# Three blocks in halves in place of four, and twelve slots per step with round ends drawn forward, in a fused convolution and two-matmul kernel

## The chip, the cores and the metric

The kernel runs on one core of a Trainium2 chip. The metric is the device time of one execution in microseconds (us). A span is the profiled part of an execution; it is mostly some 1.7 us shorter than the time. The **chain** of a profile is the work that ended last, followed back from the last instruction to what released each piece.

## The reference, cut to what matters

```python
# x: (8, 4096, 192), weight: (8 heads, 7 taps), w_in: (192, 2048), w_out: (2048, 192)
w = softmax(weight)                       # over the taps
y[b, s, :] = sum over k of w[head, k] * x_pad[b, s + k, :]   # causal, 7 taps
h = y.reshape(32768, 192) @ w_in          # first matmul
g = np.maximum(0.01 * h, h)
out = g @ w_out                           # second matmul
```

## The kernel before

The tokens are cut into 32 blocks (512 positions of two batch rows each). VectorE makes the convolution of a block (`yt`), TensorE the first matmul into PSUM (`ph`, two buffers), ScalarE (ACT in the profile) the activation into `g`, and TensorE the second matmul, which lags behind by some groups. Its outputs (`po`, `acc`) have four buffers in PSUM. A **group** is one half block or one whole block.

The first four blocks are processed as eight half blocks, so that work starts early. In this first stage, and in the first whole block after it, the second matmul has the form of `mm2_row_slot`: a **slot** is two matmuls on two halves of the array rows, and sixteen slots are a **round**. Between the two rounds of a pair of outputs the row halves swap outputs, and the program makes the swap wait for a copy on ACT (`seal`). From the second whole block on, the other form (`mm2_slot`, L545) is used, with 48 slots of four matmuls per block.

```python
NHALF = 4                                  # blocks in halves
groups = [(b, h * HT, HT) for b in range(NHALF) for h in range(2)]
groups += [(b, 0, ST) for b in range(NHALF, NBLK)]      # HT = 256, ST = 512
NSW = 2 * NHALF                            # the first whole block

def mm1(grp, u, M):                        # one unit: matmuls into ph, one activation
    ph = psum_h.tile([128, 2, ST], FP32, name="ph", tag="ph")     # bufs=2
    ...                                    # 12 matmuls of 256 or 6 of 512 columns (M=128)
    nc.scalar.activation(out=g[blk][...], in_=ph..., func=Prelu, alpha=0.01)

def mm2_row_slot(q):
    p, fc = divmod(q, 2 * NFC)             # NFC = 16: a pair has two rounds of 16 slots
    rnd, fc = divmod(fc, NFC)
    ...
    for rt in range(2):
        ins = mm2_one(rt, pair[rt ^ rnd], fc, ...)
        if first and rnd == 1:
            sync(ins, seal, "both row tiles have left these banks")
    if last and rnd == 0:
        seal_round(p, ins)                 # a copy on ACT (of the pair before, if any)
    if last and rnd == 1:
        evac_o(pair[0])                    # a copy on ACT

plan = {
    0: [0] * 4,
    NSW - 2: [16, 8, 8, 16],
    NSW - 1: [8, 8, 16, 16],
    NSW: [16, 8, 8, 16, 8, 8, 16, 16],
}
for i, grp in enumerate(groups):
    ...
    quota = plan.get(i, [16] * 4 if T == HT else [5, 5, 6, 5, 5, 6, 8, 8])
    for j in range(steps):                 # 4 steps in a half block, 8 in a whole one
        for u in range(2 * j, 2 * j + 2):
            mm1(grp, u, 128 if i <= NSW else CH)
        ...                                # whole blocks: convolution jobs of the next group
        for _ in range(quota[j]):
            mm2_row_slot(slot) if i <= NSW else mm2_slot(slot)
            slot += 1
        ...
```

The total of slots in the last three groups of the first form is 192 in 16 steps, twelve per step on average. Before, they are dealt as 16, 8, 8, 16 so that every round ends at the end of a step.

## Time and profile before

| | |
|---|---|
| time | 686.46 us (685.19 to 686.69, 3 runs) |
| TensorE busy | 99% of the span; 97% of the chain |
| ACT busy | 77%; 2% of the chain |
| VectorE busy | 71% |
| half-block group | 10.52 us with 64 slots, 9.45 us with 48 |
| whole block, later form | 20.72 us |

The last two rows come from the busy time per stretch. Each row names a stretch in us, its length, then each engine's busy time with its number of instructions (PE is TensorE, PEld its weight loads, DVE VectorE, then ACT, and POOL for GpSimd), the granted clock, the DMA share and GB/s:

```profile
51.04:61.56 10.52, 10.52 (x230) 10.52 (x226) 10.20 (x28) 9.02 (x13) 4.46 (x6) 1.00 0.66 88
72.08:81.53 9.45, 9.39 (x198) 9.20 (x194) 6.56 (x12) 8.60 (x12) 4.46 (x6) 1.00 0.84 89
192.93:213.65 20.72, 20.72 (x392) 13.20 (x388) 15.04 (x24) 15.89 (x18) 4.45 (x6) 1.00 0.60 78
```

The first is group 4 (16 slots per step), the second group 6 (16, 8, 8, 16), the third a steady whole block. In the first and third TensorE is busy the whole stretch; in the second it has 0.06 us without work.

### The profile page before, as it was taken

The numbers are of one execution on the slowest core, as the hardware profiler recorded it, in microseconds if no ns is written. First come the engines' busy times: TensorE is split into PE (matmuls) and PEld (weight loads), VectorE is DVE, ScalarE is ACT, GpSimd is POOL, SyncE is SP. The second block draws the span as 40 slices with busy tenths as digits, with TensorE's granted clock in tenths as the row PEclk, the third lists the DMA queues.
The fourth block names the chain that finished last, engine by engine and source line by source line (L and its number), as shares of the span: only waits on it lengthen the run. The fifth ranks groups of instructions, "written<-read, shape, count | busy, mean of one in ns | idle before, by whom it ended". The sixth has DMA issues, their size and how long they took to land.

```text
span 683.4 us, 27404 instructions
## 1 busy us (share of the span) xinstructions
PE 677.7 (99%) x12575; PEld 464.4 (68%) x12575; DVE 482.5 (71%) x844; ACT 524.6 (77%) x624; POOL 146.0 (21%) x204
## 2 busy tenths in 40 slices
PE   9999999999999999999999999999999999999998
PEld 6999986666666666666666666666666666666667
DVE  7979758667687667687667786676876676876612
ACT  7888998777777777777778777777777778777781
POOL 7722222222102222112221022221022220000000
PEclk9999999999999999999999999999999999999999
DMA  9975668557466566565564665574665664321123
GB/s 155 93 101 76 84 79 98 61 60 94 78 89 81 60 73 92 80 90 74 56 84 79 87 92 68 56 93 79 89 82 64 69 91 75 72 55 34 34 49 93
DMA packets 211763, 53.29 MB, mean 78 GB/s; under 512 B 205120, under 2 KB 211264, under 8 KB 211648
## 3 DMA queue, kind: packets, MB, share of 16 engines
q0 software_dynamic: 98736, 13.97, 29.9%
q1 hardware_dynamic: 112896, 37.57, 27.8%
q8 instruction: 98, 1.61, 1.0%
q14 instruction: 17, 0.14, 0.1%
q10 hardware_dynamic: 16, 0.00, 0.0%
HBM read 28.31 MB, written 25.17 MB: 78 GB/s over the span
## 4 chain that ended last, share of the span: by engine, by line
PE 97%; ACT 2%; DVE 0%; issue 0%; ACTq 0%
PE ph L456 48%; PE acc L545 41%; PE po L482 7%; ACT g L463 2%; PE acc L228 1%; ACT yt L415 0%; ACT L330 0%; ACTq L259 0%; ACT diag L387 0%; DVE yt L247 0%; ACT xt L172 0%; DVE o_sb L593 0%; DVE x_half L137 0%; ACT w L336 0%; ACT junk L330 0%
## 5 line engine op out<-in xcount | busy, mean ns | idle before, releaser
L463 ACT ACTIVATE g<-ph 128x1024 bf16<-128x1024 f32 x512 | 496.2, 1021 | 137.0 <-PE ph L456 136.6
L206 DVE SCALAR_TENSOR_TENSOR yt<-xt,wk,yt 128x512 bf16<-128x512 bf16 (+1 forms) x618 | 383.5, 702 | 0.2
L456 PE MATMUL ph<-yt,w_in 64*64 64x512 bf16 (+2 forms) x6048 | 378.4, 363 | 1.3 <-ACT g L463 0.6
L545 PE MATMUL acc<-g,w_out 64*64 64x512 bf16 x5184 | 316.5, 376 | 0.0
L456 PEld LDWEIGHTS <-w_in 64*64 64x64 bf16 (+1 forms) x6048 | 238.0, 129 | 99.1 <-issue 3.8
L545 PEld LDWEIGHTS <-w_out 64*64 64x64 bf16 x5184 | 166.7, 118 | 110.2
L82 POOL DMA_DIRECT2D x_bf<-in_x_dram x180 | 134.2, 770 | 416.2 <-DMA xt<-x_bf 309.9
L567 DVE STREAM_TRANSPOSE o_t<-acc 128x512 f32<-128x512 f32 x81 | 68.1, 885 | 169.5 <-PE acc L545 169.5
L482 PE MATMUL po<-w_out,g 64*128 64x192 bf16 (+1 forms) x1152 | 60.1, 243 | 0.0
L482 PEld LDWEIGHTS <-g 64*128 64x128 bf16 (+1 forms) x1152 | 55.6, 94 | 1.6 <-issue 0.4
L200 DVE TENSOR_SCALAR yt<-xt,wk 128x512 bf16<-128x512 bf16 (+1 forms) x103 | 28.8, 338 | 16.6 <-DMA xt<-x_bf 16.4
L555 ACT COPY junk<-junk 128x1 f32<-128x1 f32 x54 | 10.3, 192 | 3.9
L593 ACT COPY o_sb<-po 128x192 f32<-128x192 f32 x32 | 10.1, 320 | 1.3
L593 DVE COPY o_sb<-po 128x192 f32<-128x192 f32 x8 | 2.8, 357 | 6.8 <-PE po L482 3.9
L228 PE MATMUL acc<-xt,diag 64*64 64x256 bf16 x140 | 5.5, 272 | 0.3 <-ACT xt L172 0.3
L228 PEld LDWEIGHTS <-diag 64*64 64x64 bf16 x140 | 4.3, 106 | 1.4 <-issue 0.6
L324 PE MATMUL warm<-const-bfloat16-1.0 128*128 128x512 bf16 (+2 forms) x9 | 3.7, 521 | 0.8 <-PEq L695 0.8
L131 POOL DMA_DIRECT2D x_half<-in_x_dram x6 | 4.3, 757 | 0.0
L387 ACT ACTIVATE diag<-ident,whm 128x64 bf16<-128x64 bf16 x14 | 3.5, 335 | 0.2 <-DVE whm L373 0.2
L127 POOL DMA_DIRECT2D x_rows<-in_x_dram x4 | 2.9, 740 | 0.0
L330 ACT ACT_TABLE_LOAD x1 | 1.3, 1283 | 1.4 <-PEq L695 1.4
L324 PEld LDWEIGHTS <-const-bfloat16-1.0 128*128 128x128 bf16 x9 | 1.0, 122 | 2.0 <-issue 1.9
(44 smaller groups left out, 23.4 us busy)
## 6 DMA issues: line engine op xcount, KB each, us to landing
out_dram<-o_t SPq DMA_DIRECT2D x108, 192.0 KB, 4.6
x_bf<-in_x_dram POOLq DMA_DIRECT2D x180, 64.0 KB, 3.1
out_dram<-o_sb SPq DMA_DIRECT2D x16, 192.0 KB, 2.8
xt<-x_bf SPq DMA_TRANSPOSE x90, 3.7
w_out<-in_moe_w_out_dram POOLq DMA_DIRECT2D x1, 768.0 KB, 8.7
out_dram<-o_sb SPq DMA_DIRECT2D x8, 96.0 KB, 1.9
w_in<-in_moe_w_in_dram POOLq DMA_DIRECT2D x2, 256.0 KB, 4.7
x_nat<-in_x_dram SPq DMA_DIRECT2D x2, 192.0 KB, 2.5
```

The lines of the kernel that those rows point to most:

```text
L82: nc.gpsimd.dma_start(out=t[:, c, :, e, :], in_=src[2 * rp + e, :, :, c * CH : (c + 1) * CH],)
L200: lambda s=src, d=dst, c=c: nc.vector.tensor_scalar_mul(d, s, wk[:, c, 0:1])
L206: lambda s=src, d=dst, c=c, k=k: nc.vector.scalar_tensor_tensor(out=d, in0=s, scalar=wk[:, c, k : k + 1], in1=d, op0=mybir.AluOpType.mult, ...
L228: lambda k=k, p=p, a=a, ps=ps, to=to: nc.tensor.matmul(out=acc[to, :T], lhsT=diag[c][ps, p, k, :], rhs=xt[0][ps, c, a : a + T], start=(k = ...
L324: nc.tensor.matmul(out=wa[:, 0, 0:cols], lhsT=ones[:, 0:128], rhs=ones[:, 0:cols], start=True, stop=True,)
L456: nc.tensor.matmul(out=ph[m : m + M, e, i * T : (i + 1) * T], lhsT=w_in_of(f, e, c, m, m + M), rhs=y[ps, c, t0 : t0 + T], start=(c == 0), ...
L463: act = nc.scalar.activation(out=g[blk][:, nf * u : nf * (u + 1), :, t0 : t0 + T], in_=ph.rearrange("p e (i t) -> p i e t", i=nf), func=my ...
L482: return nc.tensor.matmul(out=po[m], lhsT=g[b][ps, fc, e, s * 128 : (s + 1) * 128], rhs=w_out[ps, fc, :], start=start, stop=stop,)
L545: ins = nc.tensor.matmul(out=acc2[gi, r][e * CH : (e + 1) * CH, 0:T], lhsT=w_out_of(ps, fc, r), rhs=g[b][ps, fc, e, t0 : t0 + T], start=fi ...
L555: seal = nc.scalar.copy(out=junk, in_=junk)
L567: nc.vector.transpose(out=osb[gi, 0][:, 0 : T // GB, :, r], in_=acc2.pop((gi, r))[:, 0:T].rearrange("p (j k) -> p j k", k=GB),)
L593: ins = copy(out=o_sb[:, n % 2, :], in_=po.pop(n))
```

## The change

The intent: one block fewer in halves, and no more short runs of 8 slots at the switch. Every step gets 12 slots. As rounds of 16 then end inside steps, the slots that end a round are put ahead of the step's first matmul, so that the copy on ACT is over when the next round begins.

```diff
-    NHALF = 4
+    NHALF = 3
...
-    plan = {
-        0: [0] * 4,
-        NSW - 2: [16, 8, 8, 16],
-        NSW - 1: [8, 8, 16, 16],
-        NSW: [16, 8, 8, 16, 8, 8, 16, 16],
-    }
+    plan = {0: [0] * 4}
+    for i in range(NSW - 2, NSW + 1):
+        plan[i] = [12] * (groups[i][2] // 64)
...
         for j in range(steps):
+            n, early = quota[j], 0
+            if i <= NSW and n < NFC and slot % NFC and slot % NFC + n > NFC:
+                early = NFC - slot % NFC
+            for _ in range(early):
+                mm2_row_slot(slot)
+                slot += 1
             for u in range(2 * j, 2 * j + 2):
                 mm1(grp, u, 128 if i <= NSW else CH)
...
-            for _ in range(quota[j]):
+            for _ in range(n - early):
```

## The prediction

> **What bounds the kernel now.** I read the page's busy times and the chain of work that ended last first.
>
> ```profile
> span 683.4 us, 27404 instructions
> PE 677.7 (99%) x12575; PEld 464.4 (68%) x12575; DVE 482.5 (71%) x844; ACT 524.6 (77%) x624; POOL 146.0 (21%) x204
> ...
> PE 97%; ACT 2%; DVE 0%; issue 0%; ACTq 0%
> ...
> L463 ACT ACTIVATE g<-ph 128x1024 bf16<-128x1024 f32 x512 | 496.2, 1021 | 137.0 <-PE ph L456 136.6
> ...
> L456 PE MATMUL ph<-yt,w_in 64*64 64x512 bf16 (+2 forms) x6048 | 378.4, 363 | 1.3 <-ACT g L463 0.6
> ```
>
> TensorE carries 97% of the chain, so only its issue time and its stalls count. The activation (L463) has 137.0 us idle: slack on average. But the chain gives ACT 2%, so in some places TensorE does wait for it; its idle column (0.6 us for ACT) hides this. Names from here: a **unit** is one pass of the first matmul into one of two ph buffers, followed by one activation; a **step** is two units plus its share of **slots** of the second matmul; sixteen slots are a **round**. Groups 1 to 7 are half blocks (four steps each), group 8 is the first whole block (eight steps), and from group 9 on the other form of the second matmul runs.
>
> Second, the chain in order of time, from 70 to 112 us, where the step plan is uneven (slots per step 16, 8, 8, 16, then 8, 8, 16, 16). Columns: start, length, what.
>
> ```profile
> 72.28 1.31 PE ph L456 x24
> 73.58 1.32 PE po L482 x32
> 74.91 0.67 PE ph L456 x12
> 75.57 0.02 issue
> 75.60 1.95 ACT g L463 x2
> 77.55 0.04 issue
> 77.59 0.85 PE ph L456 x12
> 78.44 0.66 PE po L482 x16
> 79.09 1.31 PE ph L456 x24
> ```
>
> ACT takes the chain at 75.60, and again at 82.42, 94.48 and 101.27: four times, each in the step after the first of two 8-slot steps. Third, the TensorE timeline there gives the size (start, length, matmuls; two matmuls make a slot):
>
> ```profile
> 74.71 1.51 PE L456 MATMUL ph<-yt,w_in 64*128 64x256 bf16 x24
> 76.02 0.86 PE L482 MATMUL po<-w_out,g 64*128 64x192 bf16 x16
> 76.68 1.76 PE L456 MATMUL ph<-yt,w_in 64*128 64x256 bf16 x24
> 78.24 0.86 PE L482 MATMUL po<-w_out,g 64*128 64x192 bf16 x16
> 78.90 1.51 PE L456 MATMUL ph<-yt,w_in 64*128 64x256 bf16 x24
> ```
>
> Two units normally take 1.31 us start to start, here 78.24 - 76.68 = 1.56: a stall of 0.25 us. The second 8-slot step is followed by no stall. So the plan of before loses 4 x 0.25 = 1.0 us in all.
>
> **What the skill says.** The Trainium skill, "TensorE: Matmul & The Clock Gate", section "Back-to-back issue gap", gives N / 2.4 + 2.5 ns as the isolated gap of a warm matmul. The trace agrees per concurrent pair: 1.31 us for 12 pairs of 256 columns is 109 ns (formula 109.2), 1.32 us for 16 slots of 192 is 82.5 (82.5), and 1.29 us for 6 pairs of 512 is 215 (215.8). "PSUM — Partial Sum Buffer", section "Engine vs sequencer instructions": ScalarE's queue is strict FIFO, and matmuls start in program order. So a unit waiting for its buffer holds everything behind it; the stall above agrees, as the 8 slots behind it start late too. "Perfetto Trace Analysis", section "Per-instruction lifecycle", says a matmul's end is estimated; this fits the waits view, where 1.0 us of stalls leaves almost no idle time. So I go by starts.
>
> **The stall rule, from the trace.** From the start of a step's first unit: 0.655 us of matmuls and 0.235 more until its activation starts (74.71 to 75.60). The second activation starts 0.92 later (76.52), lasts 1.02 (ends 77.54), and a unit that waits for it starts 0.045 later. So with s slots between the two steps, the first unit of the next step starts no earlier than 0.89 + 1.02 + 0.045 = 1.955, and its second no earlier than 0.89 + 0.92 + 1.02 + 0.045 = 2.875. Naturally the second would start at 1.31 + 0.0825 s + 0.655: with 8 slots 2.625, a stall of 0.25 as measured; with 12 slots 2.955, none; with 16, none.
>
> **The change, part by part.**
>
> 1. One block fewer in halves. The matmul columns per block are the same; the pieces get longer. A half-block group takes 10.52 us (starts 51.04, 61.56, 72.08), so a block in halves 21.04. A steady whole block takes 20.72 (130.69 to 151.41). Worth **-0.32**; the gap formula gives the same, as 2.5 ns per piece: 48 fewer pairs in the first matmul and 128 slots against 48 x 1 in the second, (48 + 80) x 2.5 = 0.32.
>
> 2. Twelve slots in every step of the last three groups (two halves, one whole block, 16 steps). The total stays 192 slots: this moves work only. Read alone, 12 slots fit the activations and would remove all four stalls, **-1.0**. But the diff also puts slots that would end a round ahead of the step's units. On TensorE there is nothing between those and the slots at the end of the previous step, so they join. Four steps run: 12 after the units; 4 ahead + 8 after; 8 ahead + 4 after; 12 after. Between pairs of units stand 12 + 4 = **16**, 8 + 8 = **16**, **4**, **12** slots. I checked this in the built order of instructions (no time in it): runs of 32, 32, 8, 24 second matmuls, four times over. Twelve per step exists in the program text alone; the engine gets a shorter run than any of before.
>
> 3. What the run of 4 costs, by the stall rule. The first unit of the next step would start at 1.31 + 0.33 = 1.64 but must wait until 1.955 (0.315); it ends at 2.61, and the second waits until 2.875 (0.265 more). Stall **0.58** per four steps. The run of 12 behind it: the two activations start at 2.845 and 3.765, the second ends at 4.785, and the second unit of the step after would start at 2.875 + 0.655 + 0.99 + 0.655 = 5.175: no stall. The 16s have more room. Four cycles: 4 x 0.58 = 2.3 against 1.0 of before: **+1.3**.
>
> 4. Round ends. Each needs a copy on ACT (0.32 us) before the next round may start. In the new order, as in the old, two units (1.31 us) follow each round end, so the copy hides: for the round end at the run of 16 the copy starts some 0.2 later and is over by 0.5. **0**.
>
> 5. The convolution on VectorE of the block that becomes whole must be done before group 6. In the trace its inputs land by 55.40; 18 operations on 512 columns take 12.0 us (75.95 to 87.96) plus 0.9 for three multiplies, so it ends near 68. Group 6 starts at 51.04 + 2 x 9.77 = 70.6. Beside other work, with 2.6 us to spare: **0**. One more block of three transposes (885 ns each) falls on a VectorE that is 71% busy: 0.
>
> Sum by groups. Old groups 6 to 8: 9.45 + 9.45 + 18.94 = 37.84 us. New groups 4 to 6: twice (4 x 1.31 + 48 x 0.0825 + 0.58) = 9.78, and 8 x 1.295 + 96 x 0.0825 + 2 x 0.59 + 0.14 (the switch of the matmul form, seen at 109.99 as 1.45 for 1.29) = 19.6, together 39.1: +1.3. With part 1: **+0.95 us**, 686.46 to 687.4.
>
> **Rivals.**
> - The plan does what its words say: stalls vanish, 686.46 - 1.0 - 0.32 = 685.1. For it: 12-slot runs would indeed not stall. Against: the built order has one 12 in four runs.
> - The whole-block convolution is late: VectorE would take the chain ahead of group 6. If the three input transposes landed 4 us later than in the old trace, TensorE would wait some 1.4 us: near 689. For it: the old trace has VectorE waiting for these transfers 16.4 us in total. Against: the order of transfers is untouched up to group 4, and 2.6 us are left.
> - A round's copy gets stuck behind the two activations, and the first slot of a round waits. The copies that come from an early round end stand in ACT's queue ahead of the new activations, so they come sooner, not later. If wrong, some 0.3 us at 12 places: near 691.
> - Nothing shows: the difference of +0.95 is about the spread of the three runs (1.5 us).
>
> **Range and chances.** The stall is arithmetic on one measured chain, so I give about 85% to a net loss of 0.5 to 1.4 us and about 10% to the first rival. Run spread adds 0.7 either way. Prediction 687.4 us, range 685.6 to 688.8. The effect is 0.14% of the time, so within 2% has 0.98, faster 0.01, slower 0.01.
>
> **What would show each step.** Right: in the new TensorE timeline, the four steps of a cycle last 2.63, 2.63, 1.95 and 2.57 us from unit start to unit start (9.78 together, for 9.45 before), with 32, 32, 8, 24 second matmuls; ACT takes the chain at four places only, each behind a run of 8 matmuls, the first near 57.2 us (51.04 + 5.26 + 0.89); group 6 starts near 70.6, and group 7 near 90.2 where old group 9 started at 109.92 (109.92 - 20.72 + 0.95 = 90.15). Wrong: the four steps take 2.3 us each (the first rival), VectorE or a transfer ahead of group 6 in the chain (the second), or slots that start late at a new round (the third).

## The result, and the profile after

The changed kernel took 688.36 us (median of 6 runs, 687.7 to 689.17) against 686.58 us of before (median of 6, 685.19 to 687.35). The ratio is 1.0031, with a 95% interval of 1.0017 to 1.0045: the same within 2%, and a little slower. A ratio is the mean time of one kernel's runs over that of the other's of the same rounds, so it is not quite the ratio of the medians.

The page of the kernel after:

```profile
span 687.3 us, 27247 instructions
PE 680.5 (99%) x12511; PEld 458.1 (67%) x12511; DVE 481.8 (70%) x826; ACT 522.9 (76%) x618; POOL 145.4 (21%) x204
...
PE 97%; ACT 2%; DMA 1%; DVE 0%; issue 0%; SPq 0%
...
L456 PE MATMUL ph<-yt,w_in 64*64 64x512 bf16 (+2 forms) x6048 | 378.1, 366 | 1.9 <-ACT g L463 0.6
```

No engine's load has changed to speak of. The idle time of TensorE ahead of the matmuls of L456 went from 1.3 to 1.9 us. The chain has a new entry, a DMA with 1%: that one is at the start of the kernel, and is taken up below. The chain in order of time at the first short run of the new plan (start, length, what):

```profile
59.34 0.67 PE ph L456 x12
60.01 0.02 issue
60.03 1.95 ACT g L463 x2
61.98 0.04 issue
62.02 0.85 PE ph L456 x12
62.87 0.99 PE po L482 x24
```

ACT still takes the chain, and in four places (60.03, 69.81, 79.55, 89.29). The TensorE timeline of the same place (start, length, what; the ends are modelled, so lengths overlap the next start, and starts are what counts; a bracket, where there is one, gives the idle time before and what ended it):

```profile
59.14 1.51 PE L456 MATMUL ph<-yt,w_in 64*128 64x256 bf16 x24
60.45 0.53 PE L482 MATMUL po<-w_out,g 64*128 64x192 bf16 x8
61.10 1.76 PE L456 MATMUL ph<-yt,w_in 64*128 64x256 bf16 x24
62.67 1.19 PE L482 MATMUL po<-w_out,g 64*128 64x192 bf16 x24
```

Behind the run of 8 matmuls (4 slots) the two units start late, at 61.10 and not 59.14 + 1.64 = 60.78, and take 62.67 - 61.10 = 1.57 us in place of 1.31. Together 0.58 us are lost: 0.32 ahead of the first unit and 0.26 ahead of the second.

The spans of the first two traces differ by 687.3 - 683.4 = 3.9 us, which is much more than four times 0.58 less four times 0.25. The starts of the groups say where it comes from:

| us | before | after | difference |
|---|---|---|---|
| start of group 4 | 51.04 | 53.88 | +2.84 |
| last three groups of the first form | 37.84 | 39.16 | +1.32 |
| from there to the end | 573.48 | 594.26 | +20.78 |
| less the two half-block groups that before has in addition | 21.04 | | -21.04 |
| sum | | | +3.9 |

The second line is the plan, lines three and four the block that is now whole. The first line was in no step of the prediction: groups 0 to 3 have the same instructions in both kernels, and yet the changed kernel reached group 4 later. That was the first question to the experiments.

### The profile page after: what moved, and what is told of

Read it like the earlier page. It is cut to its first block, busy times and chain, and to the rows that moved or that the text cites. A ratio compares the mean times of both kernels' runs of the same rounds, so it can differ in the third digit from the quotient of the medians.

```text
span 687.3 us, 27247 instructions
## 1 busy us (share of the span) xinstructions
PE 680.5 (99%) x12511; PEld 458.1 (67%) x12511; DVE 481.8 (70%) x826; ACT 522.9 (76%) x618; POOL 145.4 (21%) x204
## 3 DMA queue, kind: packets, MB, share of 16 engines
q8 instruction: 97, 1.59, 1.0%
## 4 chain that ended last, share of the span: by engine, by line
PE 97%; ACT 2%; DMA 1%; DVE 0%; issue 0%; SPq 0%
PE ph L456 47%; PE acc L545 42%; PE po L482 6%; ACT g L463 2%; PE acc L228 1%; DMA x_nat<-in_x_dram 1%; ACT yt L415 0%; PE ptr L154 0%; DVE yt L247 0%; SPq L124 0%; PE warm L324 0%; ACT x_half L137 0%; DVE o_sb L593 0%
## 5 line engine op out<-in xcount | busy, mean ns | idle before, releaser
L456 PE MATMUL ph<-yt,w_in 64*64 64x512 bf16 (+2 forms) x6048 | 378.1, 366 | 1.9 <-ACT g L463 0.6
L545 PE MATMUL acc<-g,w_out 64*64 64x512 bf16 x5376 | 328.2, 376 | 0.0
L456 PEld LDWEIGHTS <-w_in 64*64 64x64 bf16 (+1 forms) x6048 | 234.6, 130 | 103.7 <-issue 5.0
L545 PEld LDWEIGHTS <-w_out 64*64 64x64 bf16 x5376 | 172.9, 119 | 114.2
L567 DVE STREAM_TRANSPOSE o_t<-acc 128x512 f32<-128x512 f32 x84 | 70.5, 882 | 176.5 <-PE acc L545 176.5
L482 PE MATMUL po<-w_out,g 64*128 64x192 bf16 (+1 forms) x896 | 47.9, 243 | 0.0
L482 PEld LDWEIGHTS <-g 64*128 64x128 bf16 (+1 forms) x896 | 44.4, 95 | 1.6 <-issue 0.4
L593 ACT COPY o_sb<-po 128x192 f32<-128x192 f32 x24 | 7.6, 320 | 0.9
L593 DVE COPY o_sb<-po 128x192 f32<-128x192 f32 x8 | 2.8, 358 | 6.7 <-PE po L482 6.7
L228 PE MATMUL acc<-xt,diag 64*64 64x256 bf16 x140 | 7.1, 329 | 0.0
L415 ACT ACTIVATE yt<-acc,rsum 128x256 bf16<-128x256 f32 (+1 forms) x4 | 1.9, 472 | 1.9 <-PE acc L228 1.9
```

The costliest lines, as they stand in the source:

```text
L228: lambda k=k, p=p, a=a, ps=ps, to=to: nc.tensor.matmul(out=acc[to, :T], lhsT=diag[c][ps, p, k, :], rhs=xt[0][ps, c, a : a + T], start=(k = ...
L456: nc.tensor.matmul(out=ph[m : m + M, e, i * T : (i + 1) * T], lhsT=w_in_of(f, e, c, m, m + M), rhs=y[ps, c, t0 : t0 + T], start=(c == 0), ...
L482: return nc.tensor.matmul(out=po[m], lhsT=g[b][ps, fc, e, s * 128 : (s + 1) * 128], rhs=w_out[ps, fc, :], start=start, stop=stop,)
L545: ins = nc.tensor.matmul(out=acc2[gi, r][e * CH : (e + 1) * CH, 0:T], lhsT=w_out_of(ps, fc, r), rhs=g[b][ps, fc, e, t0 : t0 + T], start=fi ...
L567: nc.vector.transpose(out=osb[gi, 0][:, 0 : T // GB, :, r], in_=acc2.pop((gi, r))[:, 0:T].rearrange("p (j k) -> p j k", k=GB),)
L593: ins = copy(out=o_sb[:, n % 2, :], in_=po.pop(n))
```

## The experiments

Two theories were put against rivals. The **stall theory** is that of the prediction: what counts is how long TensorE works between two pairs of units, because both units of the next pair wait for the activations of the pair before. The **start-up** is either luck of the single execution, or belongs to the changed program. As the start-up differs from execution to execution, the table gives for each kernel's trace the start of group 2 (by then the start-up is over), the length of the last three groups of the first form, called the region, and the span less the start of group 2, which is free of the start-up.

| run | group 2 starts | region | span less start | against before | median time | ratio (95%) |
|---|---|---|---|---|---|---|
| before, first trace | 30.00 | 37.84 | 653.4 | | | |
| after, first trace | 32.84 | 39.16 | 654.5 | +1.1 | 688.36 | 1.0031 (1.0017 to 1.0045) |
| e1, before again | 32.15 | 37.85 | 653.4 | 0.0 | 686.06 | 0.9994 (0.9979 to 1.0010) |
| e2, after again | 30.02 | 39.15 | 654.5 | +1.1 | 688.01 | 1.0018 (1.0004 to 1.0031) |
| e3, three blocks in halves, old plan | 30.08 | 37.84 | 653.2 | -0.2 | 686.43 | 0.9996 (0.9979 to 1.0012) |
| e4, four blocks in halves, new plan | 31.76 | 39.15 | 654.7 | +1.3 | 688.35 | 1.0020 (1.0005 to 1.0035) |
| e5, 12 per step, no early slots | 30.11 | 41.90 | 657.2 | +3.8 | 689.14 | 1.0034 (1.0020 to 1.0048) |
| e6, runs of 16, 16, 0, 16 | 31.41 | 40.48 | 655.8 | +2.4 | 689.53 | 1.0029 (1.0015 to 1.0043) |
| e7, even runs | 32.17 | 37.19 | 652.4 | -1.0 | 686.15 | 0.9975 (0.9962 to 0.9989) |
| e8, even runs, two blocks in halves | 30.26 | 42.13 | 657.1 | +3.7 | 690.17 | 1.0047 (1.0032 to 1.0062) |
| e9, four slots between two units | 32.34 | 38.11 | 653.4 | 0.0 | 687.11 | 1.0009 (0.9995 to 1.0023) |
| e10, e7 with more warm-up matmuls | 30.11 | 37.19 | 652.5 | -0.9 | 686.17 | 0.9995 (0.9979 to 1.0011) |

All gave a correct result. e1 to e4, e5 to e8, and e9 and e10 ran on one chip each, and share its runs of before. The medians of before there were 686.66, 687.27 and 686.79.

### e1 and e2: both kernels again

No edit.

> The kernel before, unchanged, for the spread and for a second trace. Open: the first traces differ by 3.9 us of span, of which 2.8 us lie in the start-up (group 4 starts at 51.04 us before and at 53.88 after; the first input waits longer for its transfer). Theory A, start-up is luck of the transfer and of the clock: this run's group 4 starts anywhere between 51 and 54 us. Theory B, the start-up delay belongs to the changed program: this run's group 4 starts at 51.0 within 0.3, as in the first trace of before. Ratio to the runs of before 1.000 within 0.001. From the start of group 6 to the start of group 9: 37.84 us under both.

> The changed kernel, unchanged. Theory A (start-up is luck): ratio near 1.0014, the +0.95 us of the stall arithmetic, and a start-up that may differ from the 53.88 us of the first trace. Theory B (start-up delay belongs to the program): group 4 again near 53.9 us, ratio near 1.003 or above (+2 us). From group 4 to group 7: 39.1 us under both.

The start-up is luck. The kernel before now reached group 2 at 32.15 us, and the changed one at 30.02: the other way round than in the first traces. The region was the same to 0.01 us. The kernel before had executions at 685.2 us (three of six) beside others up to 687.46, and the changed kernel one at 686.44 beside five from 687.55 to 688.55. So what belongs to the change is the +1.1 us of the fifth column, not the 3.9 us between the first two traces.

The trace shows what differs. TensorE timeline of the first trace of before (quick), and then of e1 (late):

```profile
4.33 0.28 PE L324 MATMUL warm<-const-bfloat16-1.0 128*128 128x256 bf16 x1
...
5.45 3.40 PE L228 MATMUL acc<-xt,diag 64*64 64x256 bf16 x84 [0.29 <-ACT xt L172]
```

```profile
4.38 0.39 PE L324 MATMUL warm<-const-bfloat16-1.0 128*128 128x256 bf16 x1
...
5.86 5.14 PE L228 MATMUL acc<-xt,diag 64*64 64x256 bf16 x84
```

The same warm-up matmul of 256 columns takes 0.28 us in one and 0.39 in the other, and the same 84 matmuls 3.40 and 5.14 us. The Trainium skill, "TensorE: Matmul & The Clock Gate", section "What's actually happening", describes it: TensorE starts at 1.2 GHz and goes to 2.4 GHz after about 3.4 us of sustained work, measured in a window that runs freely and does not start with the kernel, so that the moment varies from run to run. The difference of 0.11 us is 256 columns at half the clock (estimate from the page's clocks: 256 / 1.2 GHz less 256 / 2.4 GHz is 0.107). In the first trace of after, the input transfer was late as well: TensorE waited 0.71 us ahead of its first transposes, a wait that neither trace above has. The profile's views of the granted clock show full speed in all of these start-ups, but only because the trace's clock records begin with the first rise and the views take what lies before as full.

The records themselves (each change of the granted clock, kept in the trace; `prof` prints only means of them) settle it. In the six traces whose group 2 starts at 30.00 to 30.26 us (before, e2, e3, e5, e8, e10), the clock rose at 3.60 to 4.28 us. In the six that start at 31.41 to 32.84 (e6, e4, e1, e7, e9, after), it rose at 8.25, 8.97, 9.78, 9.82, 10.17 and 10.27: the same order. From e6 to e9 the rise comes 1.92 us later and group 2 0.93 us later, about half, as work at half the clock would have it; after has its late input in addition. TensorE begins its warm-up at 0.84 to 0.85 us in all twelve, and the two kernels have both kinds, so no difference between the programs sets the moment. The stretches at full clock last 198, 199 or 200 times 3.413 us (in e8 14 and 185 times, with one slow window between): this agrees with a window that runs freely, and its place in an execution then decides the kind of start-up. The page's spread of the moment, 500 ns either way, is far exceeded.

Of the kernel before, 10 of all 43 executions lay within 0.15 us of its lowest time, and of the changed kernel 1 of 12. That is too few to say whether the change makes the late kind more frequent; nothing in the traces suggests a way in which it could, as TensorE's instructions up to group 4 are the same.

### e3 and e4: each half of the change alone

e3 is the kernel before with this edit:

```diff
-    NHALF = 4
+    NHALF = 3
```

> Three blocks in halves with the uneven plan of before (16, 8, 8, 16 and so on). Stall theory: the region of the last three groups costs 37.84 us as before, the rest one whole block more in place of two halves: -0.32 us, ratio 0.9995. Rival (the block that becomes whole costs more, its convolution comes late): a wait for VectorE ahead of group 6, ratio above 1.001.

e4 is the changed kernel with this edit:

```diff
-    NHALF = 3
+    NHALF = 4
```

> Four blocks in halves with the new plan (12 per step, round ends early). Stall theory: four runs of 4 slots cost 0.58 us each against four stalls of 0.25 before: region from group 6 to group 9 of 39.1 us in place of 37.84, +1.3 us, ratio 1.0019. Rival (the whole of the loss comes from the block that becomes whole): ratio 1.000.

e3 has the region of before, 37.84 us, no wait for VectorE ahead of its first whole block, and 0.2 us less in all; its lowest time is 684.81 against 685.2 of before, so 0.2 to 0.4 for -0.32 expected. e4 has the region of the changed kernel and +1.3 us. The two add up to the +1.1 of both together. So the plan costs, and the whole block gains. The ratio of e3 alone, 0.9996 with an interval of 0.0033 width, could not have told this: the start-up scatters by 2 us, and the trace had to be asked.

### e5: a true 12 per step

The changed kernel with this edit:

```diff
-            if i <= NSW and n < NFC and slot % NFC and slot % NFC + n > NFC:
-                early = NFC - slot % NFC
```

> The changed kernel without its early slots: a true 12 per step, rounds end where they fall. Stall theory: no unit waits for its buffer any more (a run of 12 leaves 0.08 us), but four of the six round ends that need a copy on ACT before the next slot (after slots 16, 80, 112, 176) fall inside a step. The copy stands behind both activations: it starts 2.73 us after the step's first unit and ends at 3.05, so the next slot starts at 3.10 and not at 1.64 (two steps, 1.46 lost each) or 1.97 (two steps, 1.13 lost each): 5.2 us. Against before: 5.2 - 1.0 - 0.3 = +3.9 us, ratio 1.0057. Rival (round ends inside a step are free, the early rule only does harm): -1.3 us, ratio 0.998.

The rival is out. The chain at the first such round end:

```profile
54.34 1.94 ACT g L463 x2
56.28 0.22 ACT o_sb L593
56.50 0.05 issue
56.55 0.83 PE po L482 x16
```

The step's first unit starts at 53.45 on TensorE. Its next slots, which the 4 slots of the old round would be through with at 55.09, start at 56.55: 3.10 after the unit, as calculated, because the copy (L593) stands behind both activations. The four steps took 3.77, 3.40, 3.73 and 3.39 us in place of 2.30. The region is 41.90 us, and the kernel 3.8 us slower than before without the start-up, as expected. The ratio of 1.0034 lies under the 1.0057 that I wrote: three of its four executions started quickly by their spans (687.2 to 687.3), and none of the nine of before on this chip did (lowest 686.39). So the early rule does its work: it replaces 5.1 us of waits by 2.3.

### e6: a run of none

The changed kernel with this plan, in which no slot is early because every round ends with a run:

```diff
-    for i in range(NSW - 2, NSW + 1):
-        plan[i] = [12] * (groups[i][2] // 64)
+    for i in range(NSW - 2, NSW + 1):
+        plan[i] = [16, 16, 0, 16] * (groups[i][2] // 256)
```

> Three blocks in halves, plan 16, 16, 0, 16 in each four steps: a larger dose of the short run, with every round end at the end of a run. Stall rule: 0.645 + 0.265 = 0.91 us in each four steps, 3.6 us in all against 1.0 of before: +2.6 - 0.3 = +2.3 us against before, ratio 1.0034; region of the last three groups 40.5 us. Rival (the loss of the change is in the mere number of switches or in the round copies): no more than the changed kernel, 39.1 us.

The TensorE timeline, where the slots between two pairs of units are missing:

```profile
57.71 1.51 PE L456 MATMUL ph<-yt,w_in 64*128 64x256 bf16 x24
59.67 1.76 PE L456 MATMUL ph<-yt,w_in 64*128 64x256 bf16 x24 [0.46 <-ACT g L463]
61.24 1.52 PE L482 MATMUL po<-w_out,g 64*128 64x192 bf16 x32
```

The second pair starts 59.67 - 57.71 = 1.96 us after the first (1.955 in the rule) and is done after 61.24 - 57.71 = 3.53, against 2.62 without waits: 0.91 lost, as calculated. The region is 40.48 us for 40.5. So there are three doses of one rule: 8 slots cost 0.25, 4 slots 0.58 and none 0.91. With a run as short as this the wait also shows as idle time.

### e9: the same slots, four of them between the two units

The changed kernel with this edit (for the steps behind a run of 4):

```diff
             for u in range(2 * j, 2 * j + 2):
                 mm1(grp, u, 128 if i <= NSW else CH)
+                if n == 12 and early == 0 and u == 2 * j and slot % NFC == 4:
+                    early = 4
+                    for _ in range(early):
+                        mm2_row_slot(slot)
+                        slot += 1
```

> The changed kernel with one thing moved: in each step behind a run of 4, four of its twelve slots go between its two units. No run gets longer, the order of the slots stays. Stall rule: the first unit still waits for its buffer (0.315 us), but the second comes 0.33 later by itself, so its 0.265 us of waiting is filled with slots: 9.51 us a cycle in place of 9.78, region of the last three groups 38.1 us in place of 39.15, -1.06 us against the changed kernel, about 0.0 against before. Rival (what the short run costs is not the buffer of the second unit, but the number of switches between the two matmuls): one switch more in each cycle, region 39.15 or more.

```profile
58.64 1.51 PE L456 MATMUL ph<-yt,w_in 64*128 64x256 bf16 x24
...
60.61 0.85 PE L456 MATMUL ph<-yt,w_in 64*128 64x256 bf16 x12
61.26 0.53 PE L482 MATMUL po<-w_out,g 64*128 64x192 bf16 x8
61.59 0.85 PE L456 MATMUL ph<-yt,w_in 64*128 64x256 bf16 x12
```

In this TensorE timeline the first unit behind the short run starts 60.61 - 58.64 = 1.97 us after the pair before (it still waits), and the second at 61.59, just 0.33 behind the end of the first: its wait is filled. The region went from 39.15 to 38.11 us, 38.1 expected, and the number of switches between the two matmuls went up. So it is the wait for the second buffer, not the switching.

### e7: even runs

The changed kernel with the early rule taken out and this plan:

```diff
-    plan = {0: [0] * 4}
-    for i in range(NSW - 2, NSW + 1):
-        plan[i] = [12] * (groups[i][2] // 64)
+    plan = {
+        0: [0] * 4,
+        NSW - 2: [16, 11, 11, 10],
+        NSW - 1: [11, 11, 10, 11],
+        NSW: [11, 10, 11, 11, 10, 16, 16, 16],
+    }
```

Only every second round end needs its copy before the next slot. Those fall on slots 16, 48, 80 and so on; 32 slots are three runs of 11, 11 and 10.

> Three blocks in halves, no early slots, plan 16, 11, 11, 10 / 11, 11, 10, 11 / 11, 10, 11, 11, 10, 16, 16, 16: every round end that needs a copy falls on the end of a run, and no run is shorter than 10. Stall rule: a run of 11 costs nothing (2.873 against 2.875), a run of 10 costs 0.08 us, four of them 0.33. Region of the last three groups 37.2 us in place of 37.84; with the block: about -1.0 us against before, ratio 0.9986, and -1.9 us against the changed kernel. Rival (the activations and copies of ACT already fill these steps, so that even runs stall too): region at 37.8 or more.

The chain has no piece of ACT any more from 23 to 110 us; the TensorE timeline shows a trace of waiting only behind the runs of 10:

```profile
60.28 1.51 PE L456 MATMUL ph<-yt,w_in 64*128 64x256 bf16 x24
61.59 1.02 PE L482 MATMUL po<-w_out,g 64*128 64x192 bf16 x20
62.41 1.59 PE L456 MATMUL ph<-yt,w_in 64*128 64x256 bf16 x24
```

1.59 in place of 1.51 is the 0.08 of the rule. The region is 37.19 us (37.2 expected), and the kernel is 1.0 us faster than before and 2.0 faster than the changed one without the start-up. Its two quickest executions, 684.16 and 684.19, compare with 685.2 of before and 686.44 of the changed kernel. The ratio of 0.9975 is better than that, and again the mix of start-ups is in it; the same plan in e10 gave 0.9995. This is the version that beats both, before by 0.15% of the time and the changed kernel by 0.3%. The traces and the quickest executions show it; of the two ratios, the interval of e10 includes 1.

### e8: one block in halves less again

e7 with `NHALF = 2` in place of 3.

> The same even plan with two blocks in halves. One block more whole: -0.32 us. But the whole-block convolution of block 2 can only start when its transposed input has landed (39.5 us in the first trace of before) and takes 12.9 us: it ends near 52, while group 4 would start near 48.2. Late-convolution theory: TensorE waits some 3 us for VectorE ahead of group 4, total +1.5 to +2.5 us against before, ratio 1.003. Rival (the convolution is hidden here too): -1.3 us, ratio 0.998.

The TensorE timeline ahead of the first whole block:

```profile
47.51 1.10 PE L482 MATMUL po<-w_out,g 64*128 64x192 bf16 x22
50.99 0.41 PE L456 MATMUL ph<-yt,w_in 64*128 64x512 bf16 x2 [2.38 <-DVE yt L206]
...
52.31 1.90 PE L456 MATMUL ph<-yt,w_in 64*128 64x512 bf16 x8 [0.25 <-DVE yt L206]
53.97 1.80 PE L482 MATMUL po<-w_out,g 64*128 64x192 bf16 x22
```

The late-convolution theory holds: the convolution ended at 52.27 and TensorE could have gone on at 48.42, so 3.9 us passed, in which only 4 matmuls were made. The total of +3.7 us is more than the +1.5 to +2.5 I wrote, for two reasons. I had taken "some 3 us" where my own numbers (52 less 48.2) gave 3.8. And TensorE went to its slow clock during the wait: the granted clock (`--windows`) is 0.50 from 52.1 to 55.4 us, and the run of 22 matmuls at 53.97 takes 55.60 - 53.97 = 1.63 us to the next start, where the same run in e7 takes 0.91 (57.15 to 58.06). The section of the skill named above says that an idle window of about 3.4 us brings the slow clock back. The clock records agree on the length: the slow stretch runs from 52.03 to 55.44 us, 3.413 us. But the window before it, from 48.61 (52.03 less 3.413), was not empty: the four matmuls at 50.99 and 51.65 lie in it, and did not keep the clock up.

### e10: can the start-up be steered?

e7 with this edit in the start-up:

```diff
     select(wps_l, 2)
-    warm(1)
+    warm(3)
```

> The even plan with two more warm-up matmuls of 256 columns just ahead of the first transposes. It asks whether the two start-ups (group 2 starts near 30.0 or near 31.4 to 32.8 us, whatever the kernel) can be steered: if the slow one comes from TensorE seeing too little work in the first 5 us, most runs should now be of the quick kind, the median near 684.2 to 684.6 and the ratio 0.996 or below. If the phase of the chip's clock window alone decides it, the mix stays and the two matmuls cost up to 0.4 us: ratio 0.998 or above. Region of the last three groups 37.2 us either way.

No. Two of six executions started quickly by their spans (682.5 and 682.6), as two of five in e7 (682.5), and the rest did not. The two matmuls cost the quick executions nothing. In the trace of e10 the clock rose at 3.60 us, as it did in e2 without them. What would make the quick kind certain stays open.

## Why the prediction was right or wrong

**The whole.** 687.4 us were predicted, in a range of 685.6 to 688.8; the median was 688.36. The predicted difference was +0.95 us. Without the start-up it is +1.1 us in both pairs of traces. The medians differ by 1.78 us, and the other 0.7 us fits the start-up: none of the first six executions of the changed kernel was of the quick kind, and two of the six of before were.

**What bounds.** Right. TensorE carries the chain in both, and the four places at which ACT takes it stayed four.

**Part 1, the block that becomes whole: -0.32.** Right; -0.26 between the first two traces (20.78 less 21.04), and -0.2 to -0.4 in e3.

**Parts 2 and 3, the short run.** Right in every number. e2 started as quickly as the first trace of before, so its times can be put beside the predicted ones directly: the four steps last 2.63, 2.63, 1.96 and 2.56 us (2.63, 2.63, 1.95, 2.57 predicted), ACT takes the chain first at 57.20 (57.2), group 6 starts at 70.62 (70.6) and group 7 at 90.21 (90.2). The prediction's sum for the three groups is 39.16 us (it writes 39.1), and 39.15 and 39.16 were measured. e6 and e9 show that the rule holds for other runs, and e4 that the plan alone makes the loss.

**Part 4, round ends: 0.** Right for the changed kernel: its chain has no copy in this stage. e5 shows what the early rule saves there.

**Part 5, the convolution: 0.** Right, and the margin was real: the whole-block convolution ended at 70.71 in the first trace of after (58.70 + 12.01), and group 6 started at 73.44, 2.7 us later (2.6 predicted). e8 shows that one block further there is no margin.

**The rivals.** The first (stalls vanish) falls by the traces. It also falls as a reading of the plan: a true 12 per step, e5, does remove the stalls but pays 5.1 us for the round ends. The late convolution is real, at `NHALF = 2`. The stuck copy is real too, without the early rule. "Nothing shows" was nearly true of the times: both intervals of the changed kernel's ratio lie just above 1, but only the traces separate 1.1 us from a start-up that scatters by 2.

**What was missing.** The prediction spoke of a spread of 0.7 us either way and put no cause to it. The start-up has a quick and a late kind, some 2 us apart, by when TensorE's clock rises, and this is twice the effect. The predicted 687.4 was built on a median that mixed both kinds. All six executions of the changed kernel were late, which puts 688.36 1 us above it, and inside the range by the width of the range, not by a cause foreseen. The traced execution of before was a quick one at 685.16, already visible in the three times of before (685.19 against 686.46 and 686.69).

## What to carry to other kernels

With two PSUM buffers between a matmul and an activation, count the TensorE work between two visits of the same buffer, not the average per step: here a pair of units needed at least 11 slots behind it, and a run of 4 cost 0.58 us even though runs of 16 and 12 stood on either side. When a rule moves work ahead of a step, look at the built order of the engine's instructions, because what is ahead of one step joins what is behind the step before. And before explaining a difference of a few tenths of a per cent, split the trace at a point that both kernels reach by the same instructions.

## What the Trainium skill lacked or had wrong

- "TensorE: Matmul & The Clock Gate", section "What's actually happening": right about the free-running window (stretches of whole multiples of 3.413 us), but it lets the moment of the rise vary by 500 ns either way, and here it lies at 3.60 to 4.28 us or at 8.25 to 10.27. It puts the ramp at under 1% of a span, which holds (2 us in 686), but this is twice the effect of the change, and two more warm-up matmuls did not steer it (2 of 6 executions quick, 2 of 5 without). Its idle window need not be empty: in e8 four matmuls in it did not keep the clock up.
- "Perfetto Trace Analysis", section "Per-instruction lifecycle": it says that a matmul's end is modelled, but not what follows for reading waits: stalls of 0.25 us show up as longer groups (1.76 for 1.51) and as almost no idle time (0.06 us in group 6 of before); even at 0.91 us lost only 0.46 is shown as idle.
- No page that I read has one number for the whole hand-over between TensorE and ScalarE through PSUM. Here: 0.235 us from where the last matmul of a unit would hand over to the next (0.655 after its start) to the start of its activation, and 0.045 us from the end of the activation to the matmul that waited for it.
- "TensorEngine Tiling (Array Packing)", section "Key Properties": it says that a change of tiling mode drains TensorE, with no figure. Here the first two units of the other mode took 1.45 us in place of 1.29 (at 109.99 us in before and at 93.11 in after); that the drain is the reason is not shown.
